# Router logits joined by a product that stays in PSUM, and row numbers counted on GpSimd

## The chip, the cores and the metric

The kernel runs on one core of a Trainium2 chip. The metric is the device time of one execution, in microseconds (us), given as the median of several runs. The core has five engines with an instruction queue each: TensorE (PE) does matrix products, VectorE (DVE) and GpSimd (POOL) do elementwise work and reductions, ScalarE (ACT) does activations and copies, SyncE (SP) issues most of the DMA transfers. Each engine runs its own queue in order, and semaphores make it wait for others. TensorE writes its results to PSUM; VectorE and ScalarE read them from there. Everything else lies in SBUF.

## The reference

Three stages follow each other. Attention with positive random features over 4 batches, 8 heads, 576 positions, 64 numbers per head; a mixture of experts (8 experts, 512 to 1024 to 512) in which each row goes to the expert with the largest logit; and a dense network of 512 to 2048 to 512 with a sigmoid gate.

```
q_p, k_p = phi(q_s), phi(k_s)      # exp(x.omega - |x|^2/2 - max) / sqrt(128)
out = (q_p @ (k_p^T v)) / (q_p . sum(k_p) + 1e-6)
x = out, as 2304 rows of 512
logits = x @ w_gate                # 8 experts
expert_idx = argmax(logits); gate_w = softmax(logits)[expert_idx]
out[mask] = gate_w * (relu(x[mask] @ w1[e]) @ w2[e])
h = x @ w_in
return (h * sigmoid(1.702 * h)) @ w_out
```

## The kernel before, in words

The work goes by batch. For each of the 4 batches (576 rows: four tiles of 128 and a tail of 64), attention is computed in blocks of four heads. A block of q or k (tile `m`, load L225 and L230) is squared on GpSimd (L239, L244) and summed on VectorE (L246), split into half-precision high and low parts (`hl`, L279 and L280), transposed by a DMA (`xT`, L281), multiplied by the features (`pr`, L316 to L323), reduced to its maximum on VectorE (L331, L340, L352: `small`, `mx`, and `qp` or `kp`) and exponentiated on ScalarE. `tq` and `qpT` (L402, L404) turn `qp` around, `num` (L416) multiplies it by `kv` (L374), and `xn` (L427) is the quotient. `tx`, `xh` and `xl` (L436, L441, L445) are its transpose, split into high and low parts for exact products: a product of full precision is three products of the parts (`mm3`, L112).

When a batch's attention is done, `route_steps` (L492) routes it. The logits come out as 16 rows, since `wgs` holds the gate's high and low parts side by side; rows 0 to 7 and 8 to 15 have to be added. Before, `lT` is turned by five transposes into `lg_ps` (L509), copied to SBUF (L514, L515), and the two halves are added on VectorE (L517). Then come the largest logit `rm` (L521), the one-hot `oh` (L523), `ex` (L526), the counts of rows per expert (`ct_ps`, L533: a product with ones), the most wanted expert `ci` (L541) and its cast `es` (L543). SyncE reads that number into a register (`values_load`, L575, TENSOR_LOAD in the queue) and loads that expert's weights (`st`, L623); ScalarE makes the high part `wh` (L645), GpSimd, in the last batch VectorE, the low part `wl` (L647). The whole batch is sent to this one expert with its gates (`dg`, `g`, `gb`, L551, L587, L590) by the products `m_ps` and `w_ps`; `y` (L736) is split into `yh` and `yl` (L739, L741), stored (L754), and loaded by the third stage (L887).

Rows that want another expert are handled by a general path behind an `If` on the count `total`. It needs for each row its expert and its gate: `ixf`, `eq` (does the row's expert agree with the batch's), `rr`, `hit`, `total` (L554 to L573). `rr` is stored to `r_dram` (L580, L583), which only the general path reads. With this data every row agrees and that path is not entered.

The program is written once in loops, with generators for attention, routing and the MoE interleaved, and a scheduler orders the instructions of every engine by priorities and estimated durations. So a changed instruction can move others on all engines. On SyncE's queue each DMA also waits until the DMA issued eight before it on the same list has landed.

Of the kernel before, what the change touches and what calls it, by code (L numbers as in the profile page):

```python
# [8 lines left out]
F32 = mybir.dt.float32  # L9
F32R = mybir.dt.float32r  # L10
F16 = mybir.dt.float16
I32 = mybir.dt.int32
U32 = mybir.dt.uint32
I64 = mybir.dt.int64
ACTF = mybir.ActivationFunctionType
ALU = mybir.AluOpType
AX = mybir.AxisListType
# [5 lines left out]
def kernel(  # L23
# [13 lines left out]
    nc = tc.nc  # L37
    B, H, S, D = q.shape
    M = omega.shape[0]
    E, DM, F1 = w1.shape  # L40
    F2 = w_in.shape[1]
    NT = B * S
    P = 128
# [113 lines left out]

    total = const.tile([P, 1], F32, name="total")
# [41 lines left out]
    for i in range(1):  # L200
        vm = att.tile([P, QH, T, D + 1], F32, name=f"vm{i}")
        vt = att.tile([P, QH, D + 1], F32, name=f"vt{i}")
        nc.gpsimd.memset(vm[:, :, :, D:D + 1], 1.0)
        nc.gpsimd.memset(vt, 0.0)
        for h in range(QH):
            p0 = (h // 2) * TAIL
            nc.gpsimd.memset(vt[p0:p0 + TAIL, h, D:D + 1], 1.0)
        vm_bufs.append(vm)
        vt_bufs.append(vt)

# [281 lines left out]
    def route_steps(b):  # L492
        yield 0
        xh, xl = xh_t[b], xl_t[b]
        lT = att.tile([2 * E, S], F32, tag="dg", name="lT", bufs=1)
# [10 lines left out]
        lg_ps = pp.tile([P, T + 1, 2, E], F32, tag="n", name="lg_ps", bufs=1)  # L506
        for t in range(T + 1):
            n = P if t < T else TAIL
            nc.tensor.transpose(  # L509
                lg_ps[:n, t].rearrange("p a e -> p (a e)"), lT[:, t * P:t * P + n], ident[:2 * E, :2 * E]  # L510
            )
        lg2 = att.tile([P, T + 1, 2, E], F32, tag="lg2", name="lg2", bufs=1)
        nc.vector.memset(lg2[:, T], 0.0)
        nc.vector.tensor_copy(lg2[:, 0:T], lg_ps[:, 0:T])  # L514
        nc.vector.tensor_copy(lg2[:TAIL, T], lg_ps[:TAIL, T])  # L515
        lg = att.tile([P, T + 1, E], F32, tag="lg", name="lg", bufs=1)
        nc.vector.tensor_tensor(out=lg, in0=lg2[:, :, 0], in1=lg2[:, :, 1], op=ALU.add)  # L517


        rm = att.tile([P, T + 1, 1], F32, tag="rm", name="rm", bufs=2)  # L520
        nc.vector.tensor_reduce(out=rm, in_=lg, axis=AX.X, op=ALU.max)  # L521
        oh = att.tile([P, T + 1, E], F32, tag="oh", name="oh", bufs=2)
        nc.vector.tensor_tensor(out=oh, in0=lg, in1=rm.to_broadcast([P, T + 1, E]), op=ALU.is_equal)  # L523
        nc.vector.memset(oh[TAIL:, T, :], 0.0)
        ex = att.tile([P, T + 1, E], F32, tag="ex", name="ex", bufs=2)
        nc.vector.tensor_tensor(  # L526
            out=ex, in0=lg, in1=rm.to_broadcast([P, T + 1, E]), op=ALU.subtract
        )
        nc.scalar.activation(out=ex, in_=ex, func=ACTF.Exp)
# [9 lines left out]
        ci = att.tile([P, 8], U32, tag="ci", name="ci", bufs=2)  # L539
        nc.vector.max(cm, ct)  # L540
        nc.vector.max_index(ci, cm, ct)  # L541
        es = att.tile([P, 1], I32, tag="es", name="es", bufs=B)
        nc.vector.tensor_copy(es, ci[:, 0:1])  # L543
# [11 lines left out]
        nc.vector.tensor_copy(cif, ci[:, 0:1])  # L555
        mx = att.tile([P, T + 1, 8], F32, tag="lmx", name="lmx", bufs=1)
        ix = att.tile([P, T + 1, 8], U32, tag="lix", name="lix", bufs=1)
        for t in range(T + 1):
# [3 lines left out]
        nc.vector.tensor_copy(ixf, ix[:, :, 0:1])  # L562
        eq = att.tile([P, T + 1, 1], F32, tag="eq", name="eq", bufs=1)
        nc.vector.tensor_scalar(out=eq, in0=ixf, scalar1=cif[:, 0:1], scalar2=None, op0=ALU.is_equal)
        nc.vector.memset(eq[TAIL:, T, :], 0.0)
        rr = att.tile([P, T + 1, 2], F32, tag="rr", name="rr", bufs=2)
        nc.vector.scalar_tensor_tensor(
            out=rr[:, :, 0:1], in0=eq, scalar=-float(2 * E), in1=ixf, op0=ALU.mult, op1=ALU.add
        )
        hit = att.tile([P, 1], F32, tag="hit", name="hit", bufs=1)  # L570
        nc.vector.tensor_reduce(out=hit, in_=eq.rearrange("p t o -> p (t o)"), axis=AX.X, op=ALU.add)
        nc.vector.tensor_tensor(out=total, in0=total, in1=hit, op=ALU.subtract)
        nc.vector.tensor_copy(rr[:, :, 1:2], gate)  # L573
# [727 lines left out]
```

## Time and profile before

| what | value |
|---|---|
| median of 3 runs | 793.82 us (791.28 to 793.97) |
| profiled execution, its own time | 793.09 us |
| its span in the trace | 791.3 us |
| busy TensorE | 96% of the span |
| busy VectorE | 57% |
| busy ScalarE | 39% |
| busy GpSimd | 22% |
| granted clock of TensorE, mean | 0.987 of full speed |

The profile is of one execution. Its engines' busy time overlaps, so their shares add to more than 100%. A row of a timeline gives the start and the duration; what stands in brackets is the idle time of the engine ahead of it and what ended that. A group "x5" is five instructions of one kind that follow each other. TensorE's granted clock is 1.00 at 2.4 GHz and 0.50 at 1.2 GHz. The routes of the four batches start at about 76, 157, 232 and 312 us.

### The profile page before, as it was taken

The numbers are of one execution on the slowest core, as the hardware profiler recorded it, in microseconds if no ns is written. First come the engines' busy times: TensorE is split into PE (matmuls) and PEld (weight loads), VectorE is DVE, ScalarE is ACT, GpSimd is POOL, SyncE is SP. The second block draws the span as 40 slices with busy tenths as digits, with TensorE's granted clock in tenths as the row PEclk, the third lists the DMA queues.
The fourth block names the chain that finished last, engine by engine and source line by source line (L and its number), as shares of the span: only waits on it lengthen the run. The fifth ranks groups of instructions, "written<-read, shape, count | busy, mean of one in ns | idle before, by whom it ended". The sixth has DMA issues, their size and how long they took to land.

```text
span 791.3 us, 14276 instructions
## 1 busy us (share of the span) xinstructions
PE 762.6 (96%) x5538; PEld 710.2 (90%) x5538; DVE 452.6 (57%) x1026; ACT 305.0 (39%) x575; POOL 177.4 (22%) x134
## 2 busy tenths in 40 slices
PE   7998999999999999979999999999999999999996
PEld 6877899999999999979997888888889999999996
DVE  5877776577764353447320656525044777777761
ACT  5545563345433341423111332244334334434330
POOL 3565297458302450201000223210000000000000
PEclk9999899999999999989999999999999999999998
DMA  5456775368624330698517999993476443444401
GB/s 158 119 141 155 220 205 140 86 155 223 152 53 136 117 93 27 208 296 244 178 30 239 332 385 322 371 386 129 139 229 210 134 134 133 134 134 133 133 28 31
DMA packets 151418, 136.01 MB, mean 172 GB/s; under 512 B 63024, under 2 KB 129840, under 8 KB 150448
## 3 DMA queue, kind: packets, MB, share of 16 engines
q1 hardware_dynamic: 139824, 116.16, 48.3%
q10 hardware_dynamic: 11520, 18.88, 6.5%
q8 instruction: 45, 0.74, 0.4%
q14 instruction: 29, 0.24, 0.1%
HBM read 83.41 MB, written 45.11 MB: 162 GB/s over the span
## 4 chain that ended last, share of the span: by engine, by line
PE 76%; DMA 11%; DVE 4%; SPq 3%; issue 2%; POOL 2%; ACT 2%; POOLq 0%; DVEq 0%; ACTq 0%
PE f_ps L112 22%; PE m_ps L112 15%; PE qa L1049 13%; PE qm L1049 7%; PE pb L1049 3%; DMA st<-in_moe_w_dram 3%; PE w_ps L112 3%; PE num L416 3%; DMA raw<-in_moe_w_in_dram 3%; DMA m<-in_k_dram 2%; PE kv_ps L374 2%; SPq L754 2%; PE pr L316 2%; DMA m<-in_q_dram 2%; PE tq L402 1%
## 5 line engine op out<-in xcount | busy, mean ns | idle before, releaser
L112 PE MATMUL f_ps<-y,wi 128*128 128x512 f32 (+1 forms) x960 | 198.4, 368 | 1.7 <-DMA y<-y_dram 1.7
L112 PEld LDWEIGHTS f_ps<-y,wi 128*128 128x128 f32 x960 | 167.0, 189 | 32.0 <-DMA y<-y_dram 2.1
L1049 PE MATMUL qa<-wo,gs 128*128 128x256 f32 x864 | 107.2, 282 | 0.0
L1049 PEld LDWEIGHTS qa<-wo,gs 128*128 128x128 f32 x864 | 104.8, 190 | 0.0
L995 ACT ACTIVATE g<-f_ps 128x512 f32<-128x512 f32 (+1 forms) x80 | 43.7, 554 | 104.3 <-PE f_ps L112 65.5
L112 PE MATMUL m_ps<-xh,wh 128*128 128x288 f32 x256 | 79.0, 309 | 3.9 <-DVE y L736 3.1
L112 PE MATMUL m_ps<-xh,wl 128*128 128x288 f32 x256 | 76.8, 300 | 0.0
L112 PE MATMUL m_ps<-xl,wh 128*128 128x288 f32 x256 | 76.6, 299 | 0.0
L647 POOL TENSOR_TENSOR wl<-st,wh 128x1024 fp32r<-128x1024 f32 x23 | 54.6, 2382 | 44.9 <-ACT wh L645 41.3
L686 DVE SCALAR_TENSOR_TENSOR h1l<-m_ps,h1h 128x288 fp32r<-128x288 f32 x64 | 28.9, 454 | 62.1 <-ACT h1h L683 62.0
L814 ACT ACTIVATE gs<-s 128x1024 fp32r<-128x1024 f32 x27 | 28.6, 1061 | 75.0 <-DVE s L1034 59.8
L331 DVE TENSOR_REDUCE small<-pr 128x4 f32<-128x512 f32 (+1 forms) x80 | 51.1, 639 | 10.0 <-PE pr L323 5.0
L1049 PE MATMUL qm<-wo,gs 128*128 128x256 f32 x432 | 54.5, 282 | 0.0
L876 POOL TENSOR_TENSOR z<-z 128x256 f32<-128x256 f32 x32 | 25.4, 814 | 127.6 <-DMA g_dram<-g 76.1
L112 PEld LDWEIGHTS m_ps<-xh,wh 128*128 128x128 f32 x256 | 48.7, 190 | 5.3 <-DVE y L736 3.6
L1049 PEld LDWEIGHTS qm<-wo,gs 128*128 128x128 f32 x432 | 52.8, 190 | 0.1
L645 ACT ACTIVATE wh<-st 128x1024 fp32r<-128x1024 f32 (+1 forms) x33 | 34.0, 1032 | 43.5 <-DMA st<-in_moe_w_dram 26.9
L815 DVE TENSOR_TENSOR gs<-gt,gs 128x1024 fp32r<-128x1024 f32 x36 | 44.2, 1226 | 10.4 <-ACT gs L814 9.9
L112 PEld LDWEIGHTS m_ps<-xl,wh 128*128 128x128 f32 x256 | 48.7, 190 | 0.3
L112 PEld LDWEIGHTS m_ps<-xh,wl 128*128 128x128 f32 x256 | 48.8, 191 | 0.0
L112 PE MATMUL m_ps<-h1h,wh 128*128 128x288 f32 x160 | 48.8, 306 | 0.0
L112 PE MATMUL m_ps<-h1h,wl 128*128 128x288 f32 x160 | 47.8, 300 | 0.0
(156 smaller groups left out, 1444.8 us busy)
## 6 DMA issues: line engine op xcount, KB each, us to landing
gt<-g_dram SPq DMA_DIRECT2D x18, 1024.0 KB, 7.2
g_dram<-g ACTq DMA_DIRECT2D x64, 256.0 KB, 5.4
st<-in_moe_w_dram SPq DMA_DIRECT2D x31, 512.0 KB, 4.5
y<-y_dram SPq DMA_DIRECT2D x8, 1024.0 KB, 8.8
raw<-in_moe_w_in_dram SPq DMA_DIRECT2D x16, 512.0 KB, 6.4
raw<-in_moe_w_out_dram SPq DMA_DIRECT2D x16, 512.0 KB, 6.3
wo<-wo_dram SPq DMA_DIRECT2D x7, 1024.0 KB, 7.8
wo_dram<-z SPq DMA_DIRECT2D x8, 768.0 KB, 7.8
```

Source lines behind the costliest of these rows:

```text
L112: ins = nc.tensor.matmul(out=ps, lhsT=a, rhs=b, start=start and n == 0, stop=stop and n == 2)
L316: nc.tensor.matmul(out=ps[:, :, h2], lhsT=xT[:, (2 * pr + h2) * 2 + t0 // 2], rhs=wbd)
L331: nc.vector.tensor_reduce(out=pm, in_=ps[:, :w], axis=AX.X, op=ALU.max, negate=on_act)
L416: nc.tensor.matmul(out=ps[:n, c, h2, :], lhsT=lhsT, rhs=kv[:, h, :])
L645: nc.scalar.activation(out=hi[:, :, s], in_=st[:, :, s], func=ACTF.Copy)
L647: eng.tensor_tensor(out=lo[:, :, s], in0=st[:, :, s], in1=f32(hi)[:, :, s], op=ALU.subtract)
L686: nc.vector.scalar_tensor_tensor(out=hl[:, f], in0=ps, scalar=0.0, in1=f32(hh[:, f]), op0=ALU.max, op1=ALU.subtract)
L814: nc.scalar.activation(out=hi, in_=src, func=ACTF.Copy)
L815: nc.vector.tensor_tensor(out=lo, in0=src, in1=f32(hi), op=ALU.subtract)
L876: nc.gpsimd.tensor_tensor(out=z[:, o], in0=z[:, a], in1=z[:, b], op=op)
L995: nc.scalar.activation(out=g, in_=ps, func=ACTF.Gelu_apprx_sigmoid)
L1049: ins = nc.tensor.matmul(out=ps, lhsT=x[:, f], rhs=w[i][:, f], start=start and f + m == 0, stop=f == NP - 1 and m == 2, skip_group_check=True,
```

## The change

Five transposes become five fp32 products of `lT` with `both`, a stacked pair of 8x8 identities, so that the sum of high and low logits is made by TensorE and stands in PSUM (128 x 5 x 8). `rm`, `oh` and `ex` read it there, and one copy (L529 of the new kernel) keeps `lg` for the general path. `lT` and the two buffers of `oh` become lasting tiles that GpSimd clears once, so the memsets of their unused rows go. The expert number is read from `ci` itself, with four buffers, and the cast `es` goes. In the general path the casts of `ci` and `ix`, `eq` with its memset, `rr`, the copy of the gate and the subtraction from `total` move from VectorE to GpSimd; the operation that made `rr` becomes two, and the sum `hit` with one subtraction becomes five subtractions.

```diff
--- before.py
+++ after.py
@@ -155,6 +155,8 @@
         nc.scalar.activation(out=wgs[:, :, 0], in_=wg, func=ACTF.Copy)
         nc.vector.tensor_tensor(out=wgs[:, :, 1], in0=wg, in1=f32(wgs[:, :, 0]), op=ALU.subtract)
 
+    both = const.tile([2 * E, E], F32, name="both")
+    nc.vector.tensor_tensor(out=both, in0=ident[:2 * E, :E], in1=ident[:2 * E, E:2 * E], op=ALU.add)
     total = const.tile([P, 1], F32, name="total")
     nc.vector.memset(total, float(NT // P))
 
@@ -207,6 +209,12 @@
             nc.gpsimd.memset(vt[p0:p0 + TAIL, h, D:D + 1], 1.0)
         vm_bufs.append(vm)
         vt_bufs.append(vt)
+
+    lT = att.tile([2 * E, (T + 1) * P], F32, name="lT")
+    nc.gpsimd.memset(lT, 0.0)
+    oh_bufs = [att.tile([P, T + 1, E], F32, name=f"oh{i}") for i in range(2)]
+    for oh in oh_bufs:
+        nc.gpsimd.memset(oh, 0.0)
 
     small = pp.tile([P, 512], F32, tag="t", name="small", bufs=1)
     ph_n = [0]
@@ -492,7 +500,6 @@
     def route_steps(b):
         yield 0
         xh, xl = xh_t[b], xl_t[b]
-        lT = att.tile([2 * E, S], F32, tag="dg", name="lT", bufs=1)
         for hf, tg in ((0, "n"), (1, "u")):
             c = slice(hf * HS, (hf + 1) * HS)
             lT_ps = pp.tile([2 * E, HS], F32, tag=tg, name="lT_ps", bufs=1)
@@ -503,29 +510,23 @@
             nc.scalar.activation(out=lT[:, c], in_=lT_ps, func=ACTF.Copy)
         yield 2.0
         yield 0
-        lg_ps = pp.tile([P, T + 1, 2, E], F32, tag="n", name="lg_ps", bufs=1)
+        lg_ps = pp.tile([P, T + 1, E], F32, tag="n", name="lg_ps", bufs=1)
         for t in range(T + 1):
-            n = P if t < T else TAIL
-            nc.tensor.transpose(
-                lg_ps[:n, t].rearrange("p a e -> p (a e)"), lT[:, t * P:t * P + n], ident[:2 * E, :2 * E]
+            nc.tensor.matmul(out=lg_ps[:, t], lhsT=lT[:, t * P:(t + 1) * P], rhs=both)
+        rm = att.tile([P, T + 1, 1], F32, tag="rm", name="rm", bufs=2)
+        nc.vector.tensor_reduce(out=rm, in_=lg_ps, axis=AX.X, op=ALU.max)
+        oh = oh_bufs[b % 2]
+        for n, t in ((P, slice(0, T)), (TAIL, slice(T, T + 1))):
+            nc.vector.tensor_tensor(
+                out=oh[:n, t], in0=lg_ps[:n, t], in1=rm[:n, t].to_broadcast([n, t.stop - t.start, E]),
+                op=ALU.is_equal,
             )
-        lg2 = att.tile([P, T + 1, 2, E], F32, tag="lg2", name="lg2", bufs=1)
-        nc.vector.memset(lg2[:, T], 0.0)
-        nc.vector.tensor_copy(lg2[:, 0:T], lg_ps[:, 0:T])
-        nc.vector.tensor_copy(lg2[:TAIL, T], lg_ps[:TAIL, T])
-        lg = att.tile([P, T + 1, E], F32, tag="lg", name="lg", bufs=1)
-        nc.vector.tensor_tensor(out=lg, in0=lg2[:, :, 0], in1=lg2[:, :, 1], op=ALU.add)
-
-
-        rm = att.tile([P, T + 1, 1], F32, tag="rm", name="rm", bufs=2)
-        nc.vector.tensor_reduce(out=rm, in_=lg, axis=AX.X, op=ALU.max)
-        oh = att.tile([P, T + 1, E], F32, tag="oh", name="oh", bufs=2)
-        nc.vector.tensor_tensor(out=oh, in0=lg, in1=rm.to_broadcast([P, T + 1, E]), op=ALU.is_equal)
-        nc.vector.memset(oh[TAIL:, T, :], 0.0)
         ex = att.tile([P, T + 1, E], F32, tag="ex", name="ex", bufs=2)
         nc.vector.tensor_tensor(
-            out=ex, in0=lg, in1=rm.to_broadcast([P, T + 1, E]), op=ALU.subtract
+            out=ex, in0=lg_ps, in1=rm.to_broadcast([P, T + 1, E]), op=ALU.subtract
         )
+        lg = att.tile([P, T + 1, E], F32, tag="lg", name="lg", bufs=1)
+        nc.vector.tensor_copy(lg, lg_ps)
         nc.scalar.activation(out=ex, in_=ex, func=ACTF.Exp)
         yield 0.5
         yield 0
@@ -536,11 +537,10 @@
         ct = att.tile([P, E], F32, tag="ct", name="ct", bufs=2)
         nc.vector.tensor_reduce(out=ct, in_=ct_ps.rearrange("p t e -> p e t"), axis=AX.X, op=ALU.add)
         cm = att.tile([P, 8], F32, tag="cm", name="cm", bufs=2)
-        ci = att.tile([P, 8], U32, tag="ci", name="ci", bufs=2)
+        ci = att.tile([P, 8], U32, tag="ci", name="ci", bufs=B)
         nc.vector.max(cm, ct)
         nc.vector.max_index(ci, cm, ct)
-        es = att.tile([P, 1], I32, tag="es", name="es", bufs=B)
-        nc.vector.tensor_copy(es, ci[:, 0:1])
+        es = ci.bitcast(I32)
         gate = att.tile([P, T + 1, 1], F32, tag="gate", name="gate", bufs=2)
         nc.vector.tensor_reduce(out=gate, in_=ex, axis=AX.X, op=ALU.add)
         nc.vector.tensor_scalar(out=gate, in0=gate, scalar1=1e-9, scalar2=None, op0=ALU.add)
@@ -552,25 +552,23 @@
                 out=dg[:n, t * P:t * P + n], in_=ident[:n, :n], func=ACTF.Copy, scale=gate[:n, t, :]
             )
         cif = att.tile([P, 1], F32, tag="cif", name="cif", bufs=2)
-        nc.vector.tensor_copy(cif, ci[:, 0:1])
+        nc.gpsimd.tensor_copy(cif, ci[:, 0:1])
         mx = att.tile([P, T + 1, 8], F32, tag="lmx", name="lmx", bufs=1)
         ix = att.tile([P, T + 1, 8], U32, tag="lix", name="lix", bufs=1)
         for t in range(T + 1):
             nc.vector.max(mx[:, t], lg[:, t])
             nc.vector.max_index(ix[:, t], mx[:, t], lg[:, t])
         ixf = att.tile([P, T + 1, 1], F32, tag="ixf", name="ixf", bufs=1)
-        nc.vector.tensor_copy(ixf, ix[:, :, 0:1])
+        nc.gpsimd.tensor_copy(ixf, ix[:, :, 0:1])
         eq = att.tile([P, T + 1, 1], F32, tag="eq", name="eq", bufs=1)
-        nc.vector.tensor_scalar(out=eq, in0=ixf, scalar1=cif[:, 0:1], scalar2=None, op0=ALU.is_equal)
-        nc.vector.memset(eq[TAIL:, T, :], 0.0)
+        nc.gpsimd.tensor_scalar(out=eq, in0=ixf, scalar1=cif[:, 0:1], scalar2=None, op0=ALU.is_equal)
+        nc.gpsimd.memset(eq[TAIL:, T, :], 0.0)
         rr = att.tile([P, T + 1, 2], F32, tag="rr", name="rr", bufs=2)
-        nc.vector.scalar_tensor_tensor(
-            out=rr[:, :, 0:1], in0=eq, scalar=-float(2 * E), in1=ixf, op0=ALU.mult, op1=ALU.add
-        )
-        hit = att.tile([P, 1], F32, tag="hit", name="hit", bufs=1)
-        nc.vector.tensor_reduce(out=hit, in_=eq.rearrange("p t o -> p (t o)"), axis=AX.X, op=ALU.add)
-        nc.vector.tensor_tensor(out=total, in0=total, in1=hit, op=ALU.subtract)
-        nc.vector.tensor_copy(rr[:, :, 1:2], gate)
+        nc.gpsimd.tensor_scalar(out=rr[:, :, 0:1], in0=eq, scalar1=-float(2 * E), scalar2=None, op0=ALU.mult)
+        nc.gpsimd.tensor_tensor(out=rr[:, :, 0:1], in0=rr[:, :, 0:1], in1=ixf, op=ALU.add)
+        for t in range(T + 1):
+            nc.gpsimd.tensor_tensor(out=total, in0=total, in1=eq[:, t], op=ALU.subtract)
+        nc.gpsimd.tensor_copy(rr[:, :, 1:2], gate)
         yield 0.5
         reg_t[b] = nc.values_load(
             es[0:1, 0:1], engines=[mybir.EngineType.SP], min_val=0, max_val=E - 1,
```

The scheduler also puts other instructions elsewhere, from the first route on. The largest part of it for VectorE is in the first route, behind `lg_ps`. Before:

```order
L514 COPY lg_1008<-lg_ps 128x64
L515 COPY lg_1008<-lg_ps 64x16
L340 TENSOR_TENSOR small<-small,sq 128x4
L517 TENSOR_TENSOR lg<-lg_1008 128x40
L340 TENSOR_TENSOR mx<-small,sq 128x4
L521 TENSOR_REDUCE rm<-lg 128x5
L559 MAX lmx<-lg 128x8
L352 TENSOR_TENSOR qp<-pr,mx 128x512
```

and now:

```order
L348 TENSOR_TENSOR small<-small,sq 128x4
L348 TENSOR_TENSOR mx<-small,sq 128x4
L360 TENSOR_TENSOR qp<-pr,mx 128x512
L517 TENSOR_REDUCE rm<-lg_ps 128x5
L339 TENSOR_REDUCE small<-pr 128x2
L520 TENSOR_TENSOR oh_135<-lg_ps,rm 128x32
L520 TENSOR_TENSOR oh_135<-lg_ps,rm 64x8
L525 TENSOR_TENSOR ex<-lg_ps,rm 128x40
L529 COPY lg<-lg_ps 128x40
```

The two copies and the add are gone, the reduction that follows `pr` (L331 before, L339 now) and `qp` (L352, L360) stand ahead of `rm`, and the copy to `lg` comes last.

A little later on VectorE the count per expert (`ct`) is turned into an expert number. Before:

```order
L537 TENSOR_REDUCE ct<-ct_ps 128x8
L340 TENSOR_TENSOR small<-small,sq 128x4
L573 COPY rr<-gate 128x5
L540 MAX cm<-ct 128x8
L340 TENSOR_TENSOR mx<-small,sq 128x4
L541 MAX_INDEX ci<-cm,ct 128x8
L246 TENSOR_REDUCE sq<-m 128x18
L352 TENSOR_TENSOR qp<-pr,mx 128x512
L543 CAST es<-ci 128x1
```

and now:

```order
L435 TENSOR_TENSOR xn<-num,rd 128x2x128
L254 TENSOR_REDUCE sq<-m 128x18
L360 TENSOR_TENSOR qp<-pr,mx 128x512
L538 TENSOR_REDUCE ct<-ct_ps 128x8
L541 MAX cm<-ct 128x8
L542 MAX_INDEX ci<-cm,ct 128x8
L339 TENSOR_REDUCE small<-pr 128x4
```

The sum of squares of the next k block (`sq`, L246 before, L254 now) and one `qp` have moved ahead of the three operations that find the number, and the cast behind it is gone.

On SyncE's queue this is the place where the number is read and the first expert weights are loaded. Before:

```order
L281 DMA_TRANSPOSE xT<-hl 128x18x128 x2
L575 TENSOR_LOAD es
L623 ISA
L623 DMA st<-in_moe_w_dram 128x4x128
L623 ISA
L623 DMA st<-in_moe_w_dram 128x4x128
L623 ISA
L623 DMA st<-in_moe_w_dram 128x4x256
```

and now:

```order
L289 DMA_TRANSPOSE xT<-hl 128x18x128 x2
L233 DMA m<-in_k_dram 128x4x256
L238 DMA m<-in_k_dram 64x2x64
L573 TENSOR_LOAD ci
L621 ISA
L621 DMA st<-in_moe_w_dram 128x4x128
L621 ISA
L621 DMA st<-in_moe_w_dram 128x4x128
L621 ISA
L621 DMA st<-in_moe_w_dram 128x4x256
```

Two loads of the next k block, which stood behind the eight weight loads, now stand ahead of the read of the number.

## Rows read from the trace of the kernel before

**Rows 1.** The page: busy time of each engine, share of the span, instructions
```profile
PE 762.6 (96%) x5538; PEld 710.2 (90%) x5538; DVE 452.6 (57%) x1026; ACT 305.0 (39%) x575; POOL 177.4 (22%) x134
```

**Rows 2.** Waits of TensorE: total us, times, longest
```profile
PE m_ps L112 <- DVE y L736: 3.1, 2, 2.2
PE w_ps L112 <- ACT wh L645: 2.3, 1, 2.3
...
PE tq L402 <- DVE xl L445: 1.3, 1, 1.3
...
PE tq L402 <- ACT qpT L404: 1.0, 1, 1.0
```

**Rows 3.** Windows of 20 us: length, busy us by engine, TensorE's clock, DMA share, GB/s
```profile
140.00:160.00 20.00, 20.00 (x186) 18.85 (x186) 11.79 (x45) 6.50 (x16) 6.70 (x5) 1.00 0.31 75
...
300.00:320.00 20.00, 20.00 (x154) 19.05 (x153) 7.97 (x44) 5.13 (x14) 1.61 (x2) 1.00 0.14 47
```

**Rows 4.** Windows of 2 us, same columns
```profile
84.00:86.00 2.00, 2.00 (x16) 1.68 (x15) 2.00 (x13) 1.62 (x6) 0.00 (x0) 0.50 0.00 1
86.00:88.00 2.00, 2.00 (x11) 1.80 (x11) 1.09 (x10) 0.27 (x1) 0.00 (x0) 0.63 1.24 283
186.00:188.00 2.00, 1.07 (x6) 1.01 (x7) 1.68 (x5) 0.17 (x2) 2.00 (x2) 0.61 0.50 144
188.00:190.00 2.00, 2.00 (x17) 2.00 (x15) 1.93 (x6) 1.67 (x4) 2.00 (x2) 0.53 0.83 263
```

**Rows 5.** Timeline of TensorE in route 0: start, us, operation, idle before it
```profile
76.44 0.45 PE L509 MATMUL lg_ps<-ident,lT 16*128 16x16 f32 x5
...
78.28 1.08 PE L416 MATMUL num<-kv,qpT 128*128 128x65 f32 x8 [0.84 <-DVE small L340]
...
80.55 1.02 PE L402 MATMUL tq<-ident,qp 128*128 128x128 f32 x4 [0.75 <-DVE qp L352]
...
83.25 0.62 PE L533 MATMUL ct_ps<-oh,ones 128*128 128x40 f32 x2 [0.83 <-DVE xn L427]
```

**Rows 6.** Timeline of VectorE in route 0
```profile
78.17 1.35 DVE L517 TENSOR_TENSOR lg<-lg 128x40 f32<-128x40 f32 x1
...
84.53 0.16 DVE L541 FIND_INDEX8 ci<-cm,ct 128x8 uint32<-128x8 f32 x1
84.66 0.75 DVE L246 TENSOR_REDUCE sq<-m 128x18 f32<-128x576 f32 x1
...
85.93 0.14 DVE L543 CAST es<-ci 128x1 int32<-128x1 uint32 x1
```

**Rows 7.** Timeline of GpSimd in route 0
```profile
77.35 2.11 POOL L239 TENSOR_TENSOR m<-m 128x1152 f32<-128x1152 f32 x1
...
96.49 4.73 POOL L647 TENSOR_TENSOR wl<-st,wh 128x1024 fp32r<-128x1024 f32 x2 [15.56 <-ACT wh L645]
```

**Rows 8.** GpSimd's operations by form: xcount, busy us, mean ns
```profile
L239 POOL TENSOR_TENSOR m<-m 128x512 f32<-128x512 f32 x5 | 5.2, 1041 | 9.9 <-PE tp L258 7.7 <-DVE small L340 2.2
...
L207 POOL MEMSET vt<- 64x1 f32 x4 | 0.3, 94 | 0.1
```

**Rows 9.** Timeline of SyncE's queue in route 0
```profile
79.87 6.76 SPq L281 DMA_TRANSPOSE xT<-hl  x2
88.01 5.96 SPq L623 DMA_DIRECT2D st<-in_moe_w_dram  x8
...
96.86 0.39 SPq L225 DMA_DIRECT2D m<-in_k_dram  x1
...
103.00 0.56 SPq L225 DMA_DIRECT2D m<-in_q_dram  x1
```

**Rows 10.** Timeline of SyncE's queue in route 3
```profile
321.50 0.38 SPq L580 DMA_DIRECT2D r_dram<-rr  x1
...
329.19 2.78 SPq L887 DMA_DIRECT2D y<-y_dram  x4
```

**Rows 11.** Timeline of VectorE in route 3
```profile
314.21 0.20 DVE L517 TENSOR_TENSOR lg<-lg 128x40 f32<-128x40 f32 x1
```

## The prediction

> **What bounds the kernel now.** The page comes first: TensorE is busy 762.6 of 791.3 us, VectorE 452.6 and GpSimd 177.4 [rows 1], so a gain or a loss has to pass through TensorE. Then the busy time by stretches of 20 us, to see where it idles near the four places at which a batch is routed: around the second and the fourth it never does, 20.00 of 20 us at the full clock [rows 3] (the third lies in a stretch that reads alike), and VectorE, busy 11.79 and 7.97 there, has slack. Only the first route lies in a stretch where TensorE waits and falls to half clock; two more such stretches lie downstream, near 186 us and 350 us, in reach of a changed order. The list of waits gives TensorE's idle time by what ended it [rows 2], the windows of 2 us show the clock [rows 4], and the timelines of the engines show who was late [rows 5, 6, 7, 9].
>
> The sum is made against the profiled execution, 793.09 us (its span of 791.3 and 1.8 around it). The median of the runs, 793.82, is 0.73 above, and I centre the forecast halfway, 0.3 above the sum.
>
> **The product of the router's logits.** Five transposes go, which took 0.45 us as five records, 0.09 each with the tail [rows 5]. Five fp32 products come. The four fp32 products of `num` stand in the trace as eight records, two each, 1.08 us or 0.135 a record [rows 5]; so the new group is ten records. By the transposes' price (16 columns, close to the 8 here) it takes 0.90, by that of `num` (65 columns) 1.35: 0.45 to 0.90 more a route. I take 0.6, nearer to the short rows. In routes 1 to 3, with TensorE full, all of it is paid: +1.7 (1.4 to 2.7). In route 0 it falls into the waits.
>
> The Trainium skill, "FP8 and Floating Point Precision", section "TensorE Precision Notes", says that true FP32 takes four passes through the array. The trace shows two records for an fp32 product [rows 5], and it decides. By four passes the group would take 20 x 0.09 - 0.45 = 1.35 more a route, +4.1 for three, and the sum would end 2.4 us higher.
>
> **VectorE in route 0.** Two copies, a memset and the add that joins the high and low logits go; five operations now read PSUM themselves. The add took 1.35 us, while GpSimd ran L239 from 77.35 to 79.46, against 0.20 in route 3, where nothing ran beside it [rows 6, 7, 11]. So 1.15 of stall and some 0.3 of copies leave the chain to the expert number. The cast `es` goes too: its number was found at 84.69 and the cast ended at 86.07, behind a reduction of 0.75 and `qp` [rows 6]. In the new order these two stand ahead of the count, so about 1.4 of this is given back, and the number is there at about 84.7 - 1.15 - 0.3 + 1.4 = 84.65, 1.4 earlier than `es`.
>
> SyncE can't use all of it. Its two DMA transposes occupy it from 79.87 to 86.63 [rows 9]; the second waits for products of TensorE, which now come earlier, since `num` and `tq` with their waits (0.84 and 0.75 [rows 5]) stand behind eight of them. Then a load of k stands ahead of the read of the number: 0.39 for the large issue [rows 9], and it waits for the reduction L246, which ends some 1.2 before the number is found (`qp` 0.68 and four short operations). It fits in, but its 512 KB share the DMA engines with the expert weights. I take 0.9 us earlier for the weights, and as much for the first MoE product.
>
> On TensorE the waits of 0.75 and 0.83 at 80.55 and 83.25 [rows 5] should shrink, since the `qp` and `xn` that end them stood behind the stalled add; the `ct` product now stands behind half of `g`, and something else of VectorE, busy 2.00 of 2 us at 84 to 86 [rows 4], is late instead. The clock is at half there: in 84 to 88 TensorE is busy 4.00 at 0.50 and 0.63 [rows 4], work of some 2.3 at the full clock, so 1.7 is lost there. I expect most of the stay at half clock to remain, because TensorE idles before the change begins too, and other waits stay. Route 0: -1.0, between 0 (all hidden behind the weights) and -3.3 (0.75 + 0.83 + 1.7).
>
> **GpSimd.** It gets thirteen small operations a route: casts, eq, a memset, a product and a sum for rr, five subtractions from total, the gate's copy. No row shows such an arithmetic operation there. A memset of one column takes 0.094 us and a product of 512 columns 1.041 [rows 8]; these of 1 to 5 columns lie between, and I take 0.2 each, near the memset: 2.6 a route, at most 13.5. In route 0 GpSimd idles 15.6 us before 96.49 [rows 7]; there nothing reaches TensorE. In route 1 the last `rr` operation stands behind two `wl` splits and one `hl`, whose consumers are weights that are split ahead of their need; what it delays is the store of `rr`, which nobody reads before the end of the MoE. I cost it at 0, 0 to +1.5 if a `wl` is late.
>
> **The order after route 0.** Near 112 us TensorE waits 1.0 for `qpT` [rows 2], because the transposed q block was late: its load was issued at 103.00 [rows 9]. With k's load moved up, q's comes closer to the weights: -0.9 (0 to -1.0). At 186 TensorE waits 1.3 for `xl` [rows 2], behind a weight split that waited for its DMA; ScalarE now does that `xh` before that split. Beside the wait, half clock in 186 to 190 (busy 1.07 at 0.61 and 2.00 at 0.53) costs 0.42 + 0.94 = 1.4 [rows 4]. All of it is -2.7; a later wait for the same weights can take it back, and beside the load of q brought forward there the store of y moves too: -1.0, from -2.7 to +1.5.
>
> In route 3 the store of `rr` stood at 321.50 ahead of stores of y, and the loads of y follow at 329.19 [rows 10]; now it waits for six small GpSimd operations behind a `yl`. These loads and the weights behind them end the waits near 350 (3.1 for y, 2.3 for `wh` [rows 2]). What the missing cast `es` gives there, the wait for `rr` takes back with some more, six operations of 0.2 and part of a `yl`: +0.5 (0 to +2).
>
> Sum: +1.7 - 1.0 + 0 - 0.9 - 1.0 + 0.5 = -0.7: 792.4 by the profiled execution, **792.7** with the shift.
>
> **The rivals.** *B, the stalls go without replacement.* The waits of route 0 and their half clock go (-3.3), the wait for `qpT` (-0.9), that for `xl` with its half clock (-2.7), against +1.7: 793.09 - 5.2 = 787.9, or 788.2. For it: each wait has one named late operation, and the change moves each. Against: VectorE is full there [rows 4], so another of its operations becomes the last.
>
> *C, slower: k's load holds up the expert weights.* It stands ahead of the read of the expert number in SyncE's queue and waits for L246 on VectorE. If L246 ends later than about 85.4, where it ended before [rows 6], less than 0.5 is won and k's 512 KB go out directly ahead of the weights: at the 283 GB/s of the window 86 to 88 [rows 4] that is 1.85 us, with 0.39 of issue at the other end; I take 1.4. TensorE then waits that much longer for its first weights and pays half clock once more (1.7 to 1.9, as at 84 to 88), while nothing is won downstream: 793.09 + 1.7 + 1.4 + 1.9 = 798.1, or 798.4. It decides when the first weight DMA is issued later than 88.01 [rows 9].
>
> *That it doesn't do what it says:* GpSimd's operations could hold VectorE as L239 held the add. The Trainium skill, "SBUF — State Buffer", has such a lock between these two engines, by which thirteen more short operations of GpSimd stall VectorE more often. The trace shows one of 1.15 beside an operation of 2.11 [rows 6, 7]. Beside thirteen operations of 0.2 stalls add up to 2.6 a route at most, off TensorE's path in routes 1 to 3. It belongs to the likeliest case.
>
> **How the numbers follow.** A (little change, 790.3 to 795.3, likeliest) 0.50; B (786 to 790.5) 0.28; C (795.5 to 801) 0.22. About 0.5%, 4 us, is what a measurement of this kernel can tell from no change: faster means under 789.9, slower over 797.8. B gives faster with four fifths of its chance, 0.22, and A adds 0.03: 0.25. C gives slower with three quarters: 0.17. The rest is 0.58. The range of 787.0 to 799.5 leaves out the ends of B and C, about 0.13.
>
> **What would show it.** In the new profile: lg_ps as ten records of 0.9 to 1.35 us in all; no L517 add; the read of the number and the first weight DMA on SyncE before 87.5 (C: after 88); the waits near 80, 83, 114 and 186 gone or smaller; full clock before 87 (B) or not (A). A wait of TensorE for `wl` near 160 to 200 us, or for y near 350 longer than 3.1, would prove the cost of GpSimd's part wrong; a product that takes over 2 us would prove the first term wrong.

## The result, and the profile after

The changed kernel takes 800.24 us in the median of 7 runs (795.53 to 803.08), the kernel before 793.65 in its 7 (791.28 to 798.26): a ratio of 1.0074, with a 95% interval of 1.0049 to 1.0099. It is slower, 0.7 us outside the forecast range and 7.5 above the forecast. All ratios leave out the few executions that ran in a slower state of the core, and they are not quotients of the two medians. The profiled execution took 801.90 us, its span 800.1.

The page's lines that answer to [rows 1], with TensorE's clock in 40 slices:

```profile
PE 767.0 (96%) x5558; PEld 713.1 (89%) x5558; DVE 445.6 (56%) x979; ACT 306.1 (38%) x575; POOL 186.1 (23%) x185
...
PEclk9979999999999999999999999999999999999999
```

VectorE lost 7.0 us of work and GpSimd gained 8.7; work was meant to move that way. But the clock's dent, which before stood in the fifth slice (80 to 100 us), now stands in the third, at 40 to 60 us. There no instruction of the router has run yet. The timelines of TensorE and of SyncE's queue in route 0 say the same; they answer to [rows 5] and [rows 9]:

```profile
83.95 1.28 PE L515 MATMUL lg_ps<-both,lT 16*128 16x8 f32 x10
```

```profile
86.55 5.58 SPq L289 DMA_TRANSPOSE xT<-hl  x2
92.22 0.53 SPq L233 DMA_DIRECT2D m<-in_k_dram  x1
92.81 0.63 SPq L238 DMA_DIRECT2D m<-in_k_dram  x1
94.44 5.64 SPq L621 DMA_DIRECT2D st<-in_moe_w_dram  x8
```

The first `lg_ps` starts at 83.95 instead of 76.44. So 7.5 us of the 8.8 by which the span grew were lost before the first changed instruction of a route. From there to the first expert weights it is 10.5 us now, 11.6 before: the route itself became shorter. The waits of TensorE, beside [rows 2]:

```profile
PE m_ps L112 <- DVE y L734: 4.5, 2, 3.0
...
PE small L446 <- DVE xl L453: 3.2, 2, 1.9
PE tq L410 <- ACT qpT L412: 2.9, 2, 2.7
...
PE m_ps L112 <- ACT wh L643: 1.7, 1, 1.7
...
PE w_ps L112 <- ACT wh L643: 1.1, 1, 1.1
```

The wait of 1.3 for `xl` near 186 us is gone (it was one of `tq`); a wait of 2.7 for `qpT` at 202.5 follows instead. New too is one of 3.2 for `xl` in two places, both ahead of route 0:

```profile
46.70 0.27 PE L446 MATMUL small<-ident,xn 64*128 64x64 f32 x1 [1.35 <-DVE xl L453]
...
75.05 0.32 PE L446 MATMUL small<-ident,xn 64*128 64x64 f32 x1 [1.88 <-DVE xl L453]
```

The windows there, of the changed kernel and then of the kernel before (length, busy us of TensorE, its weight loads, VectorE, ScalarE, GpSimd, then TensorE's clock, DMA share, GB/s):

```profile
48.00:52.00 4.00, 2.90 (x11) 1.75 (x9) 3.62 (x11) 1.14 (x4) 3.84 (x3) 0.50 0.32 70
52.00:56.00 4.00, 4.00 (x16) 3.53 (x17) 2.71 (x9) 1.54 (x3) 2.65 (x2) 0.50 0.00 0
56.00:60.00 4.00, 4.00 (x20) 3.49 (x20) 1.47 (x8) 1.97 (x6) 3.51 (x2) 0.74 0.00 0
```

```profile
48.00:52.00 4.00, 3.15 (x19) 2.53 (x20) 3.73 (x13) 2.68 (x6) 3.11 (x2) 1.00 0.25 55
52.00:56.00 4.00, 4.00 (x25) 3.10 (x23) 3.33 (x14) 2.12 (x6) 3.87 (x2) 1.00 0.00 0
56.00:60.00 4.00, 4.00 (x32) 3.57 (x31) 3.84 (x13) 1.11 (x3) 2.01 (x2) 1.00 0.70 157
```

In 48 to 60 us TensorE ran 47 products, most of them at half clock, where it had run 76 at full. Ahead of this stand the timelines of SyncE's queue and of ScalarE, changed kernel first:

```profile
35.06 2.84 SPq L289 DMA_TRANSPOSE xT<-hl  x1
38.09 0.43 SPq L233 DMA_DIRECT2D m<-in_k_dram  x1
...
45.01 1.16 ACT L287 ACTIVATE hl<-m 128x1152 f16<-128x1152 f32 x1 [4.35 <-DMA m<-in_k_dram]
...
46.18 0.20 ACT L449 ACTIVATE xh<-small 128x64 fp32r<-128x64 f32 x1
```

```profile
35.20 2.16 SPq L281 DMA_TRANSPOSE xT<-hl  x1
37.56 0.43 SPq L225 DMA_DIRECT2D m<-in_k_dram  x1
...
43.90 1.16 ACT L279 ACTIVATE hl<-m 128x1152 f16<-128x1152 f32 x1 [3.10 <-DMA m<-in_k_dram]
...
45.08 0.20 ACT L441 ACTIVATE xh<-small 128x64 fp32r<-128x64 f32 x1
```

The same transpose starts 0.14 us earlier and holds the queue 0.68 longer; the block of k behind it is used 1.1 us later. ScalarE makes `xh` behind that, 1.1 us later too; `xl` on VectorE waits for `xh` (46.42 instead of 45.31), and `small` on TensorE waits for `xl` (46.70 instead of 45.60). There TensorE idles 1.35 us, and from 48 us on its clock stands at half; a little later the kernel before idles 1.39 us once, for `qp`, and keeps the full clock. The DMA page of 34 to 48 us (40 slices of 0.35 us) shows what the transpose moved, changed kernel first:

```profile
GB/s 0 0 0 0 0 0 33 219 214 209 217 219 215 211 166 92 173 190 328 363 334 228 32 100 64 38 99 146 225 275 375 386 383 389 369 347 268 269 250 251
```

```profile
GB/s 0 0 0 0 0 0 0 198 293 289 287 285 280 121 108 117 164 328 369 360 305 65 13 20 67 122 296 374 383 351 386 325 353 340 265 266 261 140 155 157
```

While nothing else runs, 209 to 219 GB/s stand against 280 to 293. The eleven transposes as a group are slower. Over the whole span (count, ns at least, median, at most, first and last start), changed kernel first:

```profile
L289 SPq DMA_TRANSPOSE xT<-hl x11: 2714/2840/3570, 35.1 to 209.4; - x11
```

```profile
L281 SPq DMA_TRANSPOSE xT<-hl x11: 1833/1997/5067, 35.2 to 200.9; - x11
```

The fastest of the one is slower than the median of the other by 0.7 us. Up to the first `lg_ps` the order is the same on TensorE and SyncE in both kernels. Besides the clears on GpSimd and the sum `both` on VectorE, what the change moved there is where the tiles lie. The new lasting tiles, `both` (32 bytes of each partition), `lT` (2560) and two `oh` (160 each), stand ahead of `m`, `xT` and `hl`; so these lie 2912 bytes higher, 11 times 256 and 96. The built programs give the starts: `hl` at 60416 before, 236 x 256, and at 63328 now, 247 x 256 + 96.

### The profile page after: what moved, and what is told of

It reads as the page before. It is cut to its first block, busy times and chain, and to the rows that moved or that the text cites. A ratio compares the mean times of both kernels' runs of the same rounds, so it can differ in the third digit from the quotient of the medians.

```text
span 800.1 us, 14320 instructions
## 1 busy us (share of the span) xinstructions
PE 767.0 (96%) x5558; PEld 713.1 (89%) x5558; DVE 445.6 (56%) x979; ACT 306.1 (38%) x575; POOL 186.1 (23%) x185
## 4 chain that ended last, share of the span: by engine, by line
PE 78%; DMA 10%; DVE 5%; SPq 3%; ACT 2%; issue 1%; DVEq 0%; ACTq 0%
PE f_ps L112 22%; PE m_ps L112 16%; PE qa L1047 13%; PE qm L1047 6%; PE num L424 3%; PE pb L1047 3%; PE w_ps L112 3%; DMA st<-in_moe_w_dram 3%; DMA raw<-in_moe_w_in_dram 3%; PE kv_ps L382 2%; DMA m<-in_k_dram 2%; PE tq L410 2%; SPq L752 1%; PE pr L324 1%; DMA m<-in_q_dram 1%
## 5 line engine op out<-in xcount | busy, mean ns | idle before, releaser
L339 DVE TENSOR_REDUCE small<-pr 128x4 f32<-128x512 f32 (+1 forms) x80 | 51.2, 639 | 14.6 <-PE pr L331 8.3
L112 PE MATMUL m_ps<-h1l,wh 128*128 128x288 f32 x160 | 47.6, 298 | 0.0
```

What stands on the lines that cost most here:

```text
L112: ins = nc.tensor.matmul(out=ps, lhsT=a, rhs=b, start=start and n == 0, stop=stop and n == 2)
L339: nc.vector.tensor_reduce(out=pm, in_=ps[:, :w], axis=AX.X, op=ALU.max, negate=on_act)
```

## The experiments

Theory: the transposes are slow because of where a tile lies, and that is the loss. Rivals: the new instructions and their order make it, or one disturbed start. An unused tile shifts what lies behind it without changing an instruction, and the order on all engines stayed word for word that of its kernel wherever nothing else is said. The twelve runs came in three sets of four, each beside 35 runs of the kernel before (medians of 794.78, 792.16 and 794.86 us), so the ratios are what is compared.

**An unused 32 bytes in the kernel before, the size of `both`.**

```diff
+    pad_l = const.tile([P, 8], F32, name="pad_l")
     total = const.tile([P, 1], F32, name="total")
```

> The kernel before with one unused tile of 32 bytes a partition put among the constants, as large as the tile that holds the stacked identities: every instruction and its order stay as before, only the tiles of the attention, and those of the third stage's left side, lie 32 bytes higher (the blocks m, hl and xT at a multiple of 64 plus 32, before at a multiple of 64). Theory layout (the 6 us come from where the tiles lie, since every DMA transpose took 2.7 to 3.6 us instead of 1.9 to 2.4 on SyncE's queue): about 800 us (797 to 803), transposes of 2.7 us and more, and half clock on TensorE at about 47 to 59 us. Rival code (they come from the new instructions and their order) and rival chance (one disturbed start): no change, 793.7 (792 to 795.5), transposes about 2.0 us.

800.13 us, a ratio of 1.0058 (1.0029 to 1.0087). The old code alone, moved by 32 bytes, loses most of what the change lost. Its transposes:

```profile
L282 SPq DMA_TRANSPOSE xT<-hl x11: 2657/2755/4676, 34.7 to 204.6; - x11
```

The half clock at 47 to 59 us did not come in this profile; 2.23 us of waiting for `xl` came at 71 us instead, and the first `lg_ps` at 80.06. So the slow transposes were forecast rightly, and the path from them to the lost time not.

**The same 32 bytes in the changed kernel.** (Same line, behind `both`.)

> The changed kernel with one unused tile of 32 bytes put behind the stacked identities, so that m, hl and xT start at multiples of 64 bytes again; all instructions and their order as in the changed kernel. Theory layout: 793.5 us (790 to 796.5), transposes of about 2.0 us, no half clock at 47 to 59 us; what is left against the kernel before is the effect of the code itself. Rivals code and chance: 800 us as the changed kernel.

797.77 us, 1.0037 (1.0006 to 1.0067), and the expectation fell: the transposes stayed slow, although all three tiles start at multiples of 64 again.

```profile
L290 SPq DMA_TRANSPOSE xT<-hl x11: 2707/2867/3720, 35.4 to 206.9; - x11
```

**Tiles of both sides of SBUF at multiples of 64, in the old and the new kernel.**

```diff
+    padp = ctx.enter_context(tc.tile_pool(name="padp", bufs=1, side="right"))
+    pad_r = padp.tile([P, 8], F32, name="pad_r")
     moe = tc.alloc_tile_pool(name="moe", bufs=1, side="right")
...
         vt = att.tile([P, QH, D + 1], F32, name=f"vt{i}")
+        pad_a = att.tile([P, 8], F32, name="pad_a")
```

(The kernel before has the line `pad_l` of the first experiment as well.)

> The kernel before with three unused tiles of 32 bytes (constants, attention, and above the right side's tiles), so that the tiles that DMAs fill on both sides, m, hl, xT, the expert weights st, and y and the weights of the third stage, start at multiples of 64; same instructions and order. Theory layout: the transposes as before, and the loads of st and y land sooner, which stand behind the waits near 350 us: 788 to 793. If only transposes feel the address: 793.7. Rivals code and chance: 793.7.

792.65 us, 0.9991 (0.9962 to 1.002).

> The changed kernel with two unused tiles of 32 bytes (attention, and above the right side's tiles), so that the same tiles as in the aligned kernel before start at multiples of 64; same instructions and order as the changed kernel. Theory layout: within 2 us of the aligned kernel before, about 788 to 793. Rivals code and chance: 800 us.

798.06 us, 1.0035 (1.0001 to 1.0069). In both the transposes are slow, at least 2.69 and 2.68 us, so 64 is not the rule, and the two kernels are 0.4% (3.5 us) apart where 2 us at most was expected. That the old kernel still came out level has another reason: its products `qa`, first to last, took 177.3 us instead of 180.2. They took 177.0 in the changed kernel here and 177.3 in the second experiment. That comes from the unused tiles as well, and it comes back below.

**The start alone.** The kernel before with `both`, the clearing of an unused `lT` and two unused `oh` on GpSimd, and 32 unused bytes; same places as in the second experiment.

```diff
+    lT_x = att.tile([2 * E, (T + 1) * P], F32, name="lT_x")
+    nc.gpsimd.memset(lT_x, 0.0)
+    oh_x = [att.tile([P, T + 1, E], F32, name=f"ohx{i}") for i in range(2)]
+    for oz in oh_x:
+        nc.gpsimd.memset(oz, 0.0)
```

> The kernel before with only the start of the changed one: the stacked identities are made, an unused lT and two unused oh are cleared on GpSimd, and an unused 32 bytes keep m, hl and xT at multiples of 64. The order on TensorE, ScalarE and SyncE is that of the kernel before, word for word; the routing is the old one. Theory start (the clears and the place of the tiles move the start, TensorE falls to half clock at 47 to 60 us as in the profile of the changed kernel): 797 to 799, and half clock there. Rival routing (the loss is made by the new routing and the order that comes with it): 793 to 795.5, as the kernel before. The difference to the changed kernel with the same places (797.8) is then what the routing costs.

794.34 us, 1.0025 (0.9997 to 1.0052), with slow transposes (at least 2.68), the short stage of `qa` (177.1), and the clock at 0.54 and 0.61 in 48 to 56 us. So a start like that of the changed kernel comes without any of its routing. The time lies where the rival put it (793 to 795.5), but the kernel before is at 792.16 in this set, and by its ratio the run does not separate start from routing: its interval meets that of the second experiment. Its order on TensorE, ScalarE and SyncE is that of the kernel before.

**The product alone, and GpSimd's part alone.** The first is the changed kernel with the old VectorE lines from `cif` to `rr` and the 32 bytes; the second the kernel before with these lines on GpSimd:

```diff
-        nc.vector.tensor_copy(cif, ci[:, 0:1])
+        nc.gpsimd.tensor_copy(cif, ci[:, 0:1])
...
-        nc.vector.tensor_tensor(out=total, in0=total, in1=hit, op=ALU.subtract)
...
+        for t in range(T + 1):
+            nc.gpsimd.tensor_tensor(out=total, in0=total, in1=eq[:, t], op=ALU.subtract)
```

Both have orders of their own.

> The changed kernel with the general path's small operations (casts, eq, rr, hit, total, the gate's copy) back on VectorE in their old form; the product, the lasting tiles and the direct read of the expert number stay, and m, hl and xT lie at multiples of 64. If the product and the order that it brings make the loss: 797 to 799.5, with lg_ps as ten records of 1.1 to 1.3 us a route. If GpSimd's operations make it: 793 to 795.5. Theory start alone: 797 to 799.

794.67 us, 1.0029 (1.0003 to 1.0055), with slow transposes (at least 2.68) and the short `qa`. Its ratio can't be told from that of the whole change at these places (second experiment, 1.0037) or of the start alone (1.0025), so it decides nothing by itself.

> The kernel before with only the general path's small operations on GpSimd, in the form of the change; transposes, copies, add and es as before, no tile of the attention moves. If GpSimd's operations make the loss: 797 to 800. If the product or the start makes it: 793 to 795.5.

793.02 us, 1.0012 (0.9982 to 1.0041). No tile of the attention moved, and the transposes are fast (1.84 at least). GpSimd's operations alone do not make the loss.

**The kernel before, unchanged.**

> The kernel before, unchanged, for a second profile of it on this chip. Rival chance (the half clock at 47 to 60 us comes in some executions of any version): it shows here too, or the start differs from the first profile by several us with the same time in the median, 794 to 795. Theory start: TensorE keeps its full clock at 47 to 60 us here.

791.62 us, 1.0009 (0.9984 to 1.0034); TensorE kept its full clock at 48 to 60 us, and the first `lg_ps` came at 75.41.

```profile
L281 SPq DMA_TRANSPOSE xT<-hl x11: 1830/2014/5264, 35.0 to 198.7; - x11
```

So the first profile of before is no accident, and chance falls as a cause; the two differ by 1.0 us at the first `lg_ps`. By now transposes of 1.8 us at best went with one thing only: `hl` at a multiple of 256 bytes. Where they took 2.7 at best, it lay 32, 64, 96 or 128 beyond.

**The changed kernel, everything at the old places modulo 512.**

```diff
         vt = att.tile([P, QH, D + 1], F32, name=f"vt{i}")
+        pad_a = att.tile([P, 40], F32, name="pad_a")
```

> The changed kernel with an unused tile of 160 bytes at the start of the attention's tiles: m, hl and xT lie as in the kernel before, modulo 512 bytes (hl at a multiple of 256); instructions and order of the changed kernel. Theory hl (a DMA transpose is slow when its source hl does not start at a multiple of 256 bytes, and the start and all of the loss but 1 to 2 us comes from that): transposes of 1.9 to 2.3 us on SyncE's queue, first lg_ps before 78 us, and 1 to 3 us above the kernel before (794 to 796). Rival routing (the new instructions make the loss): 3 to 6 us above the kernel before, whatever the transposes.

793.06 us, 0.997 (0.9937 to 1.0003). The loss is gone, with every instruction of the change in place; the theory had still expected 1 to 3 us of it.

**The same 160 bytes, ahead of `hl` alone.**

```diff
+    moved = []
...
+        if not moved:
+            moved.append(att.tile([P, 40], F32, name="pad_h"))
         hl = att.tile([P, NB, 2, D], F16, tag="hl", name="hl", bufs=2)
```

> The changed kernel with the unused 160 bytes placed directly ahead of hl: m, xT, qp and all tiles below stay where the changed kernel has them, hl starts at a multiple of 256. If the place of hl alone decides: transposes of 1.9 to 2.3 us and the time of the kernel that moves all of them, within 2 us. If the place of xT or of the loads' target m decides: transposes of 2.7 us and more, and 4 us or more above the kernel before.

793.77 us, 0.9992 (0.9962 to 1.0023).

```profile
L292 SPq DMA_TRANSPOSE xT<-hl x11: 1844/2013/3590, 34.8 to 199.6; - x11
```

`m`, `xT` and the tiles between lie where the slow kernel has them; only `hl` and the small tiles behind it have moved, and the transposes are as fast as in the kernel before. It is the place of the transpose's source that counts.

**The best places found, for both kernels.** `hl` at a multiple of 256 again, and the third stage's left tiles moved so that they lie 64 bytes from the right ones modulo 128:

```diff
+    pad_l = const.tile([P, 8], F32, name="pad_l")
...
+        pad_a = att.tile([P, 32], F32, name="pad_a")
```

(16 and 48 numbers in the kernel before.)

> The changed kernel with 32 unused bytes among the constants and 128 at the start of the attention's tiles: hl at a multiple of 256 and, beside that, the third stage's left tiles 32 bytes higher, at a distance of 64 modulo 128 from the right ones, as in all kernels whose stage of qa took 177 us from first to last product instead of 180. Theory places: transposes as before, 177.3 us for that stage, and 3 us less than the changed kernel with hl moved: about 1 us under the kernel before (790 to 793.5). Rival chance for the 177: no difference to the kernel with hl moved.

789.30 us, 0.9936 (0.9906 to 0.9967): faster than both kernels of the change.

> The kernel before with 64 unused bytes among the constants and 192 at the start of the attention's tiles: hl at a multiple of 256 as it was, the third stage's left tiles 64 bytes higher; its own instructions and order. Theory places: 3 us under the kernel before (787.5 to 790.5), by the stage of qa alone (177.3 instead of 180.2 us). Rival chance: as the kernel before.

791.29 us, 0.9949 (0.9918 to 0.9981). The gain belongs to the places: the two intervals overlap almost wholly, and what the change itself adds can't be told from nothing. The groups of `qa` of the kernel before and of the changed one at these places (ns at least, median, at most, first and last start):

```profile
L1049 PE MATMUL qa<-wo,gs x864: 274/282/290, 604.7 to 784.9; 128*128 128x256 f32 x173
```

```profile
L1049 PE MATMUL qa<-wo,gs x864: 276/280/283, 603.0 to 780.3; 128*128 128x256 f32 x173
```

The median product takes 2 ns less, and the stage 2.9 us.

## Why the prediction was wrong

**The step that failed** is the one with which the sum begins. It took the 793.09 us of the profiled execution as given and charged only instructions and their order; the lasting tiles for `lT` and `oh` and the constant `both` had no term. They cost no time themselves (the clears take under 0.9 us of GpSimd at the start), but they moved `hl`. Moving it back in the changed kernel takes the ratio from 1.0074 to 0.9970 and 0.9992, which is the whole loss: 0.8 to 1.0% of 794 us, 6.5 to 8.3 us. In the old order a misplaced `hl` costs 0.6% (first experiment).

How the loss comes from the slow transposes is shown in part. Each holds SyncE's queue 0.7 to 0.9 us longer and lands about 0.9 later (a median of 5.0 instead of 4.1 us), and with that k's load behind the first one, and TensorE then waits for `xl`, by the rows above. For the later transposes the way to the lost time was not followed. How much its clock makes of it varies: it fell at about 48 us in five of the seven profiles with a misplaced `hl`, and in one of the seven with `hl` at a multiple of 256 (0.77 and 0.80 in 48 to 56 us, changed kernel at the old places modulo 512).

The Trainium skill, "DMA: Bandwidth & Descriptors", section "How a descriptor splits into AXI transactions", says that a transaction must start at a multiple of 256 bytes, and that a descriptor which doesn't start there has its first transaction start at the multiple below; the bytes in between are fetched and cost beats. A row of `hl` for one 128 x 128 transpose is 128 half-precision numbers, 256 bytes. If it is moved by one descriptor, which no run here shows, one transaction would become two. The runs agree in where the step is: the fastest transpose took 1.82 to 1.86 us at multiples of 256 and 2.66 to 2.71 at 32, 64, 96 and 128 beyond. By the way the page counts beats, worked out here as an estimate, 8 would become 9, 10, 11 or 12, so the time would grow with the offset; it doesn't. No run here shows the transactions themselves.

**The rest of the sum** came out near the forecast, but its terms did not. The kernels at the best places differ in the change, with fast transposes and the short `qa` in both. Read off their timelines, from the start of one step to that of the next (us):

| from, to | before | changed | difference | forecast |
|---|---|---|---|---|
| first `lg_ps` to first MoE product | 15.78 | 14.03 | -1.75 | -1.0 |
| on to the second route | 63.21 | 63.36 | +0.15 | -0.9 for q |
| second to third | 75.92 | 75.15 | -0.77 | -1.0 for 186 us, +0.6 |
| third to fourth | 80.16 | 81.24 | +1.08 | +0.6 |
| fourth to first `qa` | 292.39 | 292.97 | +0.58 | +0.5 for y, +0.6 |
| sum | 527.46 | 526.75 | -0.7 | -0.7 |

That the sums agree to a tenth is luck. The terms don't agree (and three times 0.6 is 1.8, where the forecast has 1.7), and these are single profiles: the same sum is 528.3 and 527.9 in the two of the kernel before, and 526.1 and 528.2 in the two of the changed kernel with `hl` moved. In only two rows the ranges of the old and the new order keep apart: the first is 15.78 to 17.42 in the three profiles with the old order and 14.01 to 15.51 in the three with the new, the fourth 80.16 to 80.18 and 81.24.

- *The product.* Ten records, as said. They take 1.28 us against 0.45, +0.83 in place of +0.6, inside the bounds of 0.45 to 0.90. The fourth row of the table, +1.08, is a little more than that. That two records are two passes, as the prediction took it, no row shows: a record of the fp32 product `pr` (L316, 256 columns) keeps TensorE busy 0.28 us in the mean (22.4 us for 80), one of `qa`, as wide but with operands of type float32r, 0.12 (107.2 for 864). So two records don't exclude four passes.
- *Route 0.* The stalled add is gone, and the expert's first weights are issued 9.25 us after the first `lg_ps` (85.50 and 76.25) instead of 11.3: 2.0 gained where 0.9 was forecast. The number is found 8.24 us after the first `lg_ps` (84.49), as forecast (8.21); what was priced too low is how much earlier the two transposes leave the queue, 6.9 us after it instead of 10.0. "I expect most of the stay at half clock to remain" was wrong. The windows that answer to [rows 4], in the changed kernel at the best places:

```profile
84.00:86.00 2.00, 1.81 (x21) 1.40 (x20) 1.85 (x11) 0.54 (x3) 1.04 (x5) 1.00 0.89 224
86.00:88.00 2.00, 1.78 (x16) 1.58 (x17) 1.63 (x6) 2.00 (x8) 0.87 (x5) 1.00 0.84 251
186.00:188.00 2.00, 2.00 (x17) 2.00 (x17) 1.90 (x5) 0.00 (x0) 2.00 (x2) 1.00 0.75 111
188.00:190.00 2.00, 2.00 (x21) 2.00 (x20) 1.66 (x8) 0.00 (x0) 2.00 (x3) 1.00 1.13 351
```

   The clock is full at 84 to 88 us, as rival B had it; the kernel before at its best places still has 0.50 and 0.86 there. But of B's 3.3 us only 1.75 reached the first MoE product, which waits for `wh`, and so for weights. At 186 us TensorE no longer idles or slows, also as in B, but it waits 1.1 us for `qpT` at 192, where the kernel before does not; and the half clock at 186 was absent from the second profile of the kernel before as well (1.00 from 184 to 192, beside a wait of 1.0).
- *The wait for `qpT` near 112 us* (-0.9) was of one execution: it took 1.02 us in the first profile of the kernel before, none in the second, 0.36 at its best places, and 0.51 in the changed kernel at its own.
- *GpSimd.* The operations are twelve a route, not the thirteen counted. They take 0.09 to 0.32 us each and 2.4 in all, the estimate of 0.2 holds, and nothing on TensorE waits for them. The forms of the changed kernel (count, busy us, mean ns):

```profile
L570 POOL TENSOR_TENSOR total<-total,eq 128x1 f32<-128x1 f32 x20 | 3.8, 191 | 1.0
L564 POOL TENSOR_SCALAR eq<-ixf,cif 128x5 f32<-128x5 f32 x4 | 1.3, 320 | 0.2
...
L568 POOL TENSOR_TENSOR rr<-rr,ixf 128x5 f32<-128x5 f32 x4 | 0.8, 199 | 0.0
```

- *The wait for y near 350 us* stayed: 4.5 in the changed kernel, 4.1 at its best places. By the prediction's sign, longer than 3.1, GpSimd's part would be priced wrong. But 3.1 was of one execution: the unchanged kernel's second profile has 4.1 as well, so neither the +0.5 nor its opposite is shown.

**Rival C** ended on the right side, with 798.4 near the result, by another mechanism. In the changed kernel k's load does stand in the weights' way: the transposes leave the queue at 92.13, the number is found at 92.30, and the issue of k's loads lasts to 93.44, 1.1 us longer. But against the first `lg_ps` the weights are still 1.1 us earlier than before, and with fast transposes nothing of it is left (k's loads issued by 84.50, the number found at 84.49, the weights at 85.50). Its test, "the first weight DMA is issued later than 88.01", was met by the late start, not by this cause; a test against the start of the route would have told them apart.

Open is whether, and why, a misplaced `hl` costs more in the changed kernel (0.8 to 1.0%) than in the old one (0.4 to 0.6%: 0.9991 against 0.9949 at like places, and 1.0058). These are differences between ratios whose intervals are some 0.3% wide to either side, and they overlap. In the profiles the clock fell at 48 us in all five kernels that have the clears at the start and slow transposes, and in neither of the two that have slow transposes alone. But in those two `hl` also lies 32 and 64 bytes beyond, in the five 96 and 128, and one profile each settles nothing.

## What to carry to other kernels

A change that adds a tile moves every tile allocated behind it: compare the start addresses of the two builds before charging any instruction, above all of tiles that a DMA transpose reads. When time is lost ahead of the first changed instruction, look for what the change does to places, and test it with an unused tile in the kernel before; it changes no instruction and costs one line. Look at a second profile of the same kernel before giving a wait a price: of what was charged here, the wait for `qpT` near 112 us and the half clock near 186 us were absent in the next one. Give a rival a test that is measured from the step that it speaks of, since a late start of everything will pass one in absolute time.

## What had not been expected of the hardware

- A DMA transpose of 128 x 2304 half-precision numbers within SBUF takes 1.8 to 1.9 us of its queue at best when its source starts at a multiple of 256 bytes (seven profiles) and 2.7 us when it starts 32, 64, 96 or 128 beyond (seven others); it moved 280 to 293 GB/s in the kernel before and 209 to 219 in the changed one. The place of its target, at 32 or 64 beyond multiples of 128, made no difference.
- The products `qa` on TensorE took 279 to 280 ns in the median instead of 282 to 283 when the tiles of the left side lay 64 bytes from those of the right, modulo 128, and not at 0 or 32: in all seven profiles with 64 (177 us for the stage) and none of the seven others (180 us). Two of them were forecast before they ran. Which of the tiles counts, and why, was not tried.
